# Linear attention and a feed-forward block in one planned program: loads, preparations and transposes get their own tokens in the order, and the order is rewritten

## The chip, the core and the metric

The kernel runs on one core of one Trainium2 chip. The metric is the device time of one execution in microseconds (us). The engines are named as the profile names them: PE is TensorE (its weight loads are PEld), DVE is VectorE, ACT is ScalarE, POOL is GpSimd, SP is SyncE, which here only issues DMAs.

## What is computed

Linear attention with a decay per head comes first, for 4 batches, 8 heads, 768 positions and 64 channels, in blocks of 64 positions; its output, laid out as 3072 tokens of 512 channels, goes through a feed-forward block of width 2048 with a "snake" activation. The reference, shortened:

```python
for b in range(nb):                       # 12 blocks of 64 positions
    intra = einsum(qb, kb) * Dmask        # decay lam ** (i - j), causal
    out[b] = intra @ vb + (qb * lam_pow) @ kv_state
    kv_state = lam_block * kv_state + (kb * rev_pow).T @ vb
x = out.transpose(0, 2, 1, 3).reshape(3072, 512)
h = x @ w_in                              # 512 -> 2048
g = h + sin(alpha * h) ** 2 / (alpha + 1e-9)
y = g @ w_out                             # 2048 -> 512
```

## The kernel before

**Units and chunks.** A unit is 256 positions of one batch with all 8 heads; there are 12 units, 0 to 11, and two units make a chunk of 512 tokens, of which there are 6. For each unit three loads bring q, k and v as float32 (`load_unit`, issued on SP in halves for units 0 and 1 and whole, 512 KB each, after that). Each of the three has two halves by head group, and `uscale` prepares each half: k is cast to bfloat16 (line 509), q and v are multiplied by a table of powers of lam (line 523). Units 0 to 3 are then transposed by PE into a PSUM bank and copied out (`upiece_T`, lines 539 and 548); units 4 to 11 are transposed by a DMA that SP issues (`upiece_D`, line 555).

**Attention pieces.** Line 578 issues the small matmuls of the attention: scores S, sums Z for the state, and outputs O. DVE masks the scores into `Smu` (lines 658 and 767) and adds the state `Zs` (671 and 778); the state is cast into `Zu` (674 and 781); O is cast into `xT`, the feed-forward input (688 and 788). For units 4 on, `upair` joins the S and Z of one unit with the O of the unit before; it uses seven of the eight PSUM banks.

**Feed-forward.** An A piece makes 512 columns of PSUM with four matmuls of 128x512 (`unit_A`, line 811) or with eight of 128x256 (`unit_A2`, line 845, written h in the order). ACT takes the sine (821 and 855), POOL or ACT the square (826 and 860, or 825 and 859), and DVE multiplies and adds into `gT` (828, and 863 twice for an h), which also frees the bank. A B piece is four matmuls of 128x512 (`unit_B`, line 876); four of them, written b chunk.tile.quarter, make 128 tokens of output, which ACT copies (890) and stores. There are 96 A pieces and 96 B pieces. The weights arrive by DMAs on POOL's queue, the first 512 columns of w_in by SP as float32 (`ws`) with a cast (line 424).

**What sets the order.** `_Plan` records every operation with a guessed length, its reads and its writes, and then picks operations one by one: the one that can start first, and among those the one recorded first. `HEAD` is the list for units 0 and 1. `ORDER` is a list of tokens for the rest: a and h make an A piece, b a B piece, s passes over a free bank, g makes the next attention piece. Loads, preparations (`uprep`, all six halves of a unit) and DMA transposes of units 4 on are recorded by the list `ahead`, in a fixed sequence, as soon as enough attention pieces have been made. An operation with several possible engines goes to the one that the plan sees finished first, after an addition per engine. Until 26 us of the plan, PE's waits are filled with idle matmuls (line 950).

## Time and profile before

| what | value |
|---|---|
| median of 3 runs | 216.12 us (216.10 to 216.44) |
| profiled execution | 216.58 us |
| its span in the profile | 214.8 us |
| time outside the span | 1.78 us |
| PE, DVE, ACT, POOL busy | 205.0, 136.6, 143.5, 93.9 us |
| DMA read and written | 27.28 MB, 6.29 MB |

The page has the busy time of each engine, then the span in 40 slices, the chain that ended last, and groups of instructions by line. An "idle before" with an arrow names what released the engine. A busy PE row ends where its pipelined last matmul is modelled to end, so rows of PE that follow each other overlap by some 0.17 us.

### The profile page before, as it was taken

How to read it: one execution, taken by the hardware profiler on the slowest of the kernel's cores; microseconds unless marked ns; L12 is line 12 of the kernel's file. 1: busy time of each engine (PE TensorE's matmuls, PEld its weight loads, DVE VectorE, ACT ScalarE, POOL GpSimd, SP SyncE). 2: the span in 40 equal slices, each digit the busy share in tenths (PEclk: the TensorE clock that was granted, in tenths of full speed). 3: DMA queues.
4: the chain of work that ended last, by engine and by line, in shares of the span. 5: the costliest groups of instructions: out<-in, count | busy, mean ns of one | idle time of the engine just before them, and what ended most of it. 6: DMA issues, size and time to landing. Idle time of an engine off the chain costs nothing.

```text
span 214.8 us, 5435 instructions
## 1 busy us (share of the span) xinstructions
PE 205.0 (95%) x2290; PEld 114.9 (53%) x2290; DVE 136.6 (64%) x225; ACT 143.5 (67%) x264; POOL 93.9 (44%) x106
## 2 busy tenths in 40 slices
PE   4999998999997998999999999999999999999995
PEld 1355756455644755547655558855454444444454
DVE  2697677796779964969985557846656556543000
ACT  2466887655788835777955867937758699686141
POOL 2555573752759656447985405912300530110000
PEclk9999999999999999999999999999999999999999
DMA  4999999999999999999999815011011000001134
GB/s 108 298 309 234 206 255 258 252 265 344 297 202 289 271 179 318 178 283 218 277 251 268 99 49 101 2 42 62 0 52 49 0 0 3 0 2 49 52 146 148
DMA packets 62986, 34.45 MB, mean 160 GB/s; under 512 B 18273, under 2 KB 60017, under 8 KB 62961
## 3 DMA queue, kind: packets, MB, share of 16 engines
q1 hardware_dynamic: 55632, 24.25, 50.3%
q0 software_dynamic: 3696, 3.67, 10.3%
q10 hardware_dynamic: 3632, 6.17, 8.6%
q8 instruction: 18, 0.29, 0.6%
q14 instruction: 8, 0.06, 0.1%
HBM read 27.28 MB, written 6.29 MB: 156 GB/s over the span
## 4 chain that ended last, share of the span: by engine, by line
PE 78%; DMA 11%; POOL 3%; SPq 3%; ACT 2%; issue 1%; DVE 0%; POOLq 0%
PE bank L876 38%; PE bank L811 18%; PE bank L845 13%; PE bank L578 7%; DMA w<-in_moe_w_in_dram 5%; DMA k<-in_k_dram 3%; SPq L385 3%; DMA q<-in_q_dram 3%; POOL u L826 2%; PE bank L539 1%; POOL w L385 1%; ACT t L821 1%; POOL qkv L523 1%; ACT osb L890 0%; DVE gT L828 0%
## 5 line engine op out<-in xcount | busy, mean ns | idle before, releaser
L876 PE MATMUL bank<-w,gT 128*128 128x512 bf16 (+1 forms) x400 | 89.6, 371 | 1.0 <-ACT osb L890 0.7
L876 PEld LDWEIGHTS bank<-w,gT 128*128 128x128 bf16 x400 | 38.0, 98 | 41.6 <-ACT osb L890 1.2
L828 DVE SCALAR_TENSOR_TENSOR gT<-u,rinv,bank 128x512 bf16<-128x512 bf16 x56 | 40.7, 744 | 22.0 <-ACT u L825 13.4
L811 PE MATMUL bank<-xT,w 128*128 128x512 bf16 x224 | 53.1, 379 | 0.8 <-DVE gT L828 0.5
L821 ACT ACTIVATE t<-bank,alpha 128x512 bf16<-128x512 f32 x56 | 37.4, 685 | 12.2 <-PE bank L811 11.4
L863 DVE SCALAR_TENSOR_TENSOR gT<-u,rinv,bank 128x256 bf16<-128x256 bf16 x80 | 34.3, 475 | 12.8 <-POOL u L860 7.3
L845 PE MATMUL bank<-xT,w 128*128 128x256 bf16 x320 | 38.7, 273 | 0.2 <-DVE gT L828 0.2
L855 ACT ACTIVATE t<-bank,alpha 128x256 bf16<-128x256 f32 x80 | 32.9, 474 | 6.6 <-PE bank L845 5.0
L811 PEld LDWEIGHTS bank<-xT,w 128*128 128x128 bf16 x224 | 21.5, 98 | 25.7 <-DVE gT L828 1.0
L845 PEld LDWEIGHTS bank<-xT,w 128*128 128x128 bf16 x320 | 30.5, 98 | 8.2 <-ACT xT L788 1.5
L860 POOL TENSOR_TENSOR u<-t 128x512 bf16<-128x512 bf16 x25 | 26.0, 1056 | 17.8 <-ACT t L855 17.7
L826 POOL TENSOR_TENSOR u<-t 128x512 bf16<-128x512 bf16 x19 | 20.2, 1069 | 29.9 <-ACT t L821 19.6
L890 ACT COPY osb<-bank 128x512 f32<-128x512 f32 (+1 forms) x25 | 14.2, 568 | 21.9 <-PE bank L876 21.9
L767 DVE TENSOR_TENSOR Smu<-bank,masku 128x1024 bf16<-128x1024 f32 x16 | 18.9, 1219 | 13.6 <-PE bank L578 13.6
L825 ACT ACTIVATE u<-t 128x512 bf16<-128x512 bf16 x37 | 23.3, 630 | 1.8 <-DVE gT L828 0.6
L523 POOL TENSOR_TENSOR qkv<-v,Lv 128x512 bf16<-128x512 f32 x15 | 17.4, 1167 | 12.8 <-PE bank L578 10.9
L523 POOL TENSOR_TENSOR qkv<-q,Lq 128x512 bf16<-128x512 f32 x13 | 15.0, 1159 | 11.5 <-DMA q<-in_q_dram 11.5
L788 ACT CAST xT<-bank 128x512 bf16<-128x512 f32 x14 | 9.8, 740 | 9.5 <-PE bank L578 9.5
L950 PE MATMUL bank<-masku,ident 128*128 128x512 bf16 x33 | 11.2, 452 | 2.7 <-DVE masku L461 2.7
L658 DVE TENSOR_TENSOR Smu<-bank,masku 128x1024 bf16<-128x1024 f32 x8 | 9.7, 1223 | 3.3 <-PE bank L578 3.2
L509 ACT CAST qkv<-k 128x512 bf16<-128x512 f32 x11 | 6.8, 617 | 6.0 <-DMA k<-in_k_dram 6.0
L578 PE MATMUL bank<-qkT,Zu 64*64 64x128 bf16 x160 | 10.3, 221 | 0.3
(55 smaller groups left out, 142.0 us busy)
## 6 DMA issues: line engine op xcount, KB each, us to landing
out_dram<-osb ACTq DMA_DIRECT2D x23, 256.0 KB, 2.1
k<-in_k_dram SPq DMA_DIRECT2D x10, 512.0 KB, 6.5
q<-in_q_dram SPq DMA_DIRECT2D x10, 512.0 KB, 7.2
v<-in_v_dram SPq DMA_DIRECT2D x10, 512.0 KB, 8.0
w<-in_moe_w_out_dram POOLq DMA_DIRECT2D x4, 512.0 KB, 9.4
w<-in_moe_w_in_dram POOLq DMA_DIRECT2D x3, 512.0 KB, 11.4
k<-in_k_dram SPq DMA_DIRECT2D x4, 256.0 KB, 5.4
v<-in_v_dram SPq DMA_DIRECT2D x4, 256.0 KB, 5.4
```

The lines of the kernel that those rows point to most:

```text
L523: emit = lambda e: e.tensor_tensor(dst, src, tab, ALU.mult)
L578: ins = e.matmul(to, w, x, start=(b, c) not in seen, stop=True, skip_group_check=True)
L811: ins = e.matmul(ps[hb][:, c0:c1], w1[:, kc, 128 * m:128 * (m + 1)], xT[x][:, kc, c0:c1], start=(kc == 0 and c0 == lo), stop=(kc == NKC - ...
L821: op("ACT", lambda e: e.activation(t16[ju][:, w], ps[hb][:, w], ACTF.Sin, scale=alpha[:, m:m + 1]), 0.69 * f, [bank(hb), "alpha"], [("t16" ...
L825: lambda e: (e.activation(u16[ju][:, w], t16[ju][:, w], ACTF.Square) if e is nc.scalar else e.tensor_tensor(u16[ju][:, w], t16[ju][:, w], ...
L826: e.tensor_tensor(u16[ju][:, w], t16[ju][:, w], t16[ju][:, w], ALU.mult)), 0,
L828: op("DVE", lambda e: e.scalar_tensor_tensor(out=gT[g][:, m, w], in0=u16[ju][:, w], scalar=rinv[:, m:m + 1], in1=ps[hb][:, w], op0=ALU.mul ...
L845: ins = e.matmul(ps[hb][:, 256 * i:256 * i + 256], w1[:, kc, 128 * (m + i):128 * (m + i + 1)], xT[x][:, kc, lo:lo + 256], start=(kc == 0 a ...
L855: op("ACT", lambda e, i=i: e.activation(t16[ju][:, 256 * i:256 * i + 256], ps[hb][:, 256 * i:256 * i + 256], ACTF.Sin, scale=alpha[:, m + ...
L860: e.tensor_tensor(u16[ju][:, :], t16[ju][:, :], t16[ju][:, :], ALU.mult)), 0,
L863: op("DVE", lambda e, i=i: e.scalar_tensor_tensor(out=gT[g][:, m + i, lo:lo + 256], in0=u16[ju][:, 256 * i:256 * i + 256], scalar=rinv[:, ...
L876: ins = e.matmul(ps[ob][:, w], gT[g][:, m, 128 * s4:128 * (s4 + 1)], w2[:, m, w], start=(m == 0), stop=(m == NM - 1),)
```

## The change

Numbers for the planner: later or shorter landings of unit loads, 0.9 us in place of 0.68 us for a q or v scale on DVE from unit 2 on, 1.1 us in place of 1.05 us on POOL, 1.8 us and 3.2 us in place of 1.45 us and 2.5 us for a DMA transpose. The additions that steer an operation away from an engine come from a list, `late_by`, set by a token G in `HEAD`. The list `ahead` goes; in its place the order has tokens l (next unit's loads), p (next unit's preparation) and d (next unit's two DMA transposes). `HEAD` and `ORDER` are new.

```diff
-                        lat=(2.7 if u < 4 else 5.0) if g is None else 2.9, ...
+                        lat=(2.7 if u < 2 else 3.7 if u < 4 else 3.9) if g is None else 2.9, ...
-            HEAD = """lk00 lv00 lq00 lk01 k01:POOL lv01 lq01 v01:POOL q00:POOL lk10 k00:DVE ...
+            HEAD = """lq01 lk00 lv00 lv10 v00:POOL k00:POOL lq00 lv01 Tk00:2ACT v01:POOL lk01 q01:DVE G:-1,7,8,2,6,6,12
-                    long = {"POOL": 1.05 if u > 1 else 1.1, "DVE": 0.68}
+                    long = {"POOL": 1.1, "DVE": 0.9 if u > 1 else 0.68}
-                op("SP", lambda e: e.dma_start_transpose(qkT[:, sl, :, :], flat), 1.45,
+                op("SP", lambda e: e.dma_start_transpose(qkT[:, sl, :, :], flat), 1.8,
...
-                   dma=f"qkT{sl}", runs=16, lat=2.5, issue=1.3)
+                   dma=f"qkT{sl}", runs=16, lat=3.2, issue=1.3)
-                        op((("ACT", 0.4, 0.0), ("POOL", 0.4, 0.0)),
+                        op((("ACT", 0.4, late_by[6]), ("POOL", 0.4, 0.0)),
-                        op((("ACT", 0.74, 0.4), ("DVE", 0.72, 0.0)),
+                        op((("ACT", 0.74, late_by[5]), ("DVE", 0.72, 0.0)),
-                op((("POOL", 1.05 * f, 0.0), ("ACT", 0.6 * f, 0.2)),
+                op((("POOL", 1.05 * f, 0.0), ("ACT", 0.62 * f, late_by[0])),
-                op((("POOL", 1.05, 0.0), ("ACT", 0.6, 0.3)),
+                op((("POOL", 1.05, 0.0), ("ACT", 0.62, late_by[1])),
-            ORDER = """h0.1.6 h0.1.0 b0.0.0 h0.1.2 h0.0.6 a0.4 b0.2.0 a0.5 h0.1.14 h0.1.8 s s s h0.0.14 s s g ...
+            ORDER = """p h0.1.0 a0.4 s s h0.1.2 a0.5 g a0.6 a0.7 b0.2.0 b0.0.0 s h0.1.8 s s h0.1.14 h0.0.8 s s ...
-                    uscale(u, which, g, (("ACT", 0.2), ("POOL", 0.0), ("DVE", 0.5)) if which == "k" else (("POOL", 0.0), ("DVE", 0.5)))
+                    uscale(u, which, g, (("ACT", late_by[2]), ("POOL", 0.0), ("DVE", late_by[3])) if which == "k" else (("POOL", 0.0), ("DVE", late_by[4])))
-                while ahead and ahead[0][0] <= done:
-                    ahead.pop(0)[1]()
+                elif kind == "l":
+                    load_unit(next(loads), "kqv")
+                elif kind == "p":
+                    uprep(next(preps))
+                elif kind == "d":
+                    u = next(turns)
+                    upiece_D(u, "k")
+                    upiece_D(u, "q")
```

Three places show what this does to the engines. The first is PE at the end of the head, where the feed-forward begins. L578 is the attention of unit 1, L950 (L961 after) an idle matmul, L845 and L811 are A pieces, L876 a B piece. Before:

```order
L578 MATMUL bank<-qkT 64x128 x16
L950 MATMUL bank<-masku,ident 128x512
L845 MATMUL bank<-xT,w 128x256 x8
L578 MATMUL bank<-Smu,qkv 64x128 x16
L578 MATMUL bank<-qkT,Zu 64x128 x4
L578 MATMUL bank<-Smu,qkv 64x128 x16
L578 MATMUL bank<-qkT,Zu 64x128 x4
L845 MATMUL bank<-xT,w 128x256 x32
L811 MATMUL bank<-xT,w 128x512 x4
L876 MATMUL bank<-w,gT 128x512 x4
```

And now:

```order
L578 MATMUL bank<-qkT 64x128 x16
L961 MATMUL bank<-masku,ident 128x512 x7
L578 MATMUL bank<-Smu,qkv 64x128 x16
L578 MATMUL bank<-qkT,Zu 64x128 x4
L961 MATMUL bank<-masku,ident 128x512
L578 MATMUL bank<-Smu,qkv 64x128 x16
L578 MATMUL bank<-qkT,Zu 64x128 x4
L845 MATMUL bank<-xT,w 128x256 x24
L811 MATMUL bank<-xT,w 128x512 x8
L845 MATMUL bank<-xT,w 128x256 x8
```

The A piece that stood ahead of unit 1's last two attention outputs has moved behind them, and eight idle matmuls stand there instead of one.

The second place is POOL's queue in the head, with the semaphores that each row waits for; dma_uq11 is the landing of q, unit 1, second half, and ws0 and ws256 are the two parts of the first w_in columns. Before:

```order
L385 DMA w1<-in_moe_w_in_dram 128x4x512 [waits dma_uq11]
L385 DMA w2<-in_moe_w_out_dram 128x4x512
L385 DMA w1<-in_moe_w_in_dram 128x4x512 [waits dma_uv11]
L523 TENSOR_TENSOR qkv<-v32_1,Lv 128x512 [waits dma_uv10]
L385 DMA w1<-in_moe_w_in_dram 128x4x512 [waits dma_ws256]
L385 DMA w2<-in_moe_w_out_dram 128x4x512
```

And now:

```order
L523 TENSOR_TENSOR qkv<-q32_1,Lq 128x2x4x64 [waits dma_uq10]
L385 DMA w1<-in_moe_w_in_dram 128x4x512
L523 TENSOR_TENSOR qkv<-q32_1,Lq 128x2x4x64 [waits dma_uq11]
L385 DMA w1<-in_moe_w_in_dram 128x4x512
L385 DMA w1<-in_moe_w_in_dram 128x4x512 [waits dma_ws0]
L385 DMA w2<-in_moe_w_out_dram 128x4x512
L523 TENSOR_TENSOR qkv<-v32_1,Lv 128x512 [waits dma_uv11]
L385 DMA w2<-in_moe_w_out_dram 128x4x512
```

The first weight load has moved ahead; it is now the last quarter of w_in, `w1[3]`, for whose landing SP's load of unit 2 waits. The last v half of unit 1 is prepared behind four weight loads.

The third place is POOL around unit 4's scores, where units 5 and 6 are prepared. The digit of k32, q32 and v32 is the load buffer: 2 is unit 5 and 0 unit 6. Before:

```order
L860 TENSOR_TENSOR u16_0<-t16_0 128x512 [waits done_ACT]
L509 CAST qkv<-k32_2 128x2x4x64 [waits dma_uk2]
L523 TENSOR_TENSOR qkv<-q32_2,Lq 128x2x4x64 [waits dma_uq2]
L826 TENSOR_TENSOR u16_2<-t16_2 128x512 [waits done_ACT]
L826 TENSOR_TENSOR u16_1<-t16_1 128x512 [waits done_ACT]
L523 TENSOR_TENSOR qkv<-v32_2,Lv 128x512 [waits dma_uv2]
L826 TENSOR_TENSOR u16_3<-t16_3 128x512 [waits done_DVE,done_ACT]
L826 TENSOR_TENSOR u16_0<-t16_0 128x512 [waits done_DVE,done_ACT]
L826 TENSOR_TENSOR u16_2<-t16_2 128x512 [waits done_DVE,done_ACT]
L509 CAST qkv<-k32_0 128x2x4x64 [waits dma_uk0]
L523 TENSOR_TENSOR qkv<-q32_0,Lq 128x2x4x64 [waits dma_uq0]
```

And now:

```order
L860 TENSOR_TENSOR u16_1<-t16_1 128x512 [waits done_ACT]
L523 TENSOR_TENSOR qkv<-q32_2,Lq 128x2x4x64 [waits dma_uq2]
L860 TENSOR_TENSOR u16_0<-t16_0 128x512 [waits done_ACT]
L523 TENSOR_TENSOR qkv<-v32_2,Lv 128x512 [waits dma_uv2]
L860 TENSOR_TENSOR u16_2<-t16_2 128x512 [waits done_ACT]
L826 TENSOR_TENSOR u16_1<-t16_1 128x512 [waits done_ACT]
L826 TENSOR_TENSOR u16_3<-t16_3 128x512 [waits done_DVE,done_ACT]
L860 TENSOR_TENSOR u16_1<-t16_1 128x512 [waits done_ACT]
L781 CAST Zu_0<-Zs 128x256 [waits done_DVE]
L860 TENSOR_TENSOR u16_3<-t16_3 128x512 [waits done_ACT]
L860 TENSOR_TENSOR u16_1<-t16_1 128x512 [waits done_DVE,done_ACT]
L509 CAST qkv<-k32_0 128x2x4x64 [waits dma_uk0]
```

Unit 5's k is now prepared ahead of this stretch, its v ahead of most squares, and unit 6's k behind five more squares.

Over the whole program, counted in the order, POOL has 15 casts of k (10 before), 32 scales of q and v (28), 47 squares (44) and 14 casts of the state (9); ACT has 3 casts of k (11), 6 casts of the state (11) and 49 squares (52); DVE has 6 casts of k (3), 16 scales (20), and both casts of `ws`, which ACT had. A pieces of the h kind are 42 (40), of the a kind 54 (56). PE's matmuls are the same in number otherwise, but for 38 idle ones (33).

More of the change, by code (lines that the diff above doesn't have):

```diff
@@ L918, in _ @@
+            late, late_by = {}, [0.0] * 7
             for item in HEAD:
@@ L944, in _ @@
                     free = [int(x) for x in what]
+                elif kind == "G":
+                    late_by[:] = [int(x) / 10 for x in what.split(",")]
             load_w2(2, [last["w1", 2]])
@@ L979, in _ @@
                 outs_at[u - 1] = len(pieces) if u > U0 else outs_at[u - 1]
[L980 to L987 removed]
+            load_unit(2, "kqv", None, [last["w1", 3]])
+            load_w2(3, [last["k", 2]])
+            load_unit(3, "kqv")
+            loads, preps, turns = (iter(range(x, NU)) for x in (4, 2, UD))
             done, todo = 0, ORDER.split()
             for i, token in enumerate(todo):
[L990 to L991 removed]
                 kind, arg = token[0], [int(x) for x in token[1:].split(".") if x]
@@ L1023, in _ @@
                         free.append(held.pop((c, t)))
-            assert done == len(pieces) and not ahead
+            assert done == len(pieces)
             P.filler = (spin, ("masku", "ident"), 26.0)
```

63 lines of the change are left out of this document (31 added, 32 removed).

## The prediction

> **What bounds it now.** First the page: which engine is full, and what the last chain is made of.
>
> ```profile
> PE 205.0 (95%) x2290; PEld 114.9 (53%) x2290; DVE 136.6 (64%) x225; ACT 143.5 (67%) x264; POOL 93.9 (44%) x106
> PE 78%; DMA 11%; POOL 3%; SPq 3%; ACT 2%; issue 1%; DVE 0%; POOLq 0%
> ```
>
> PE is busy for 95% of the span and makes 78% of the chain; the DMA share is the head, before the feed-forward can begin. So the time is a start, then PE's fixed work, then PE's stalls, then the tail. The timeline of PE dates the start and the first wait for unit 2, the chain the end:
>
> ```profile
> 19.84 1.04 PE L845 MATMUL bank<-xT,w 128*128 128x256 bf16 x8
> 22.08 3.73 PE L845 MATMUL bank<-xT,w 128*128 128x256 bf16 x32
> ...
> 34.69 0.61 PE L539 MATMUL bank<-ident,qkv 128*128 128x128 bf16 x8 [0.55 <-ACT qkv L509]
> ...
> 124.66 3.45 PE bank L876 x16
> ...
> 195.75 16.46 PE bank L876 x92
> ```
>
> One A piece runs at 19.84; from 22.08 to 195.75 + 16.46 = 212.21 (190.1 us) PE runs the other 191 pieces and the attention of units 2 to 11. Four pieces take 3.45 us, so one takes 0.863. The stretches and PE's own waits behind 35 us show where it stalls:
>
> ```profile
> 22.00:35.14 13.14, 12.23 (x91) 8.06 (x92) 9.35 (x20) 10.41 (x22) 7.66 (x8) 1.00 1.20 244
> ...
> 55.73:75.00 19.27, 17.86 (x178) 11.10 (x177) 16.91 (x27) 16.88 (x34) 13.88 (x15) 1.00 1.19 260
> 75.00:95.00 20.00, 19.06 (x288) 10.31 (x287) 13.94 (x24) 12.45 (x24) 11.30 (x13) 1.00 1.15 238
> ...
> PE bank L876 <- ACT osb L890: 0.7, 1, 0.7
> PE bank L811 <- DVE gT L828: 0.5, 1, 0.5
> PE bank L578 <- DVE gT L863: 0.4, 1, 0.4
> PE bank L811 <- issue: 0.3, 1, 0.3
> PE bank L578 <- DVE gT L828: 0.2, 1, 0.2
> PE bank L845 <- DVE gT L828: 0.2, 1, 0.2
> ```
>
> The columns are the stretch's length, then the busy time of PE, PEld, DVE, ACT and POOL. PE is short by 1.41 us in 55.73:75 and by 0.94 us in 75:95, with six waits (2.3 us). A wait really costs some 0.17 us more than its idle time, since the row ahead of it ends late by that (19.84 + 1.04 reaches past the 0.865 us of its eight matmuls): 2.35 + 6 x 0.17 = **3.4 us behind 35 us**. From 22.08 to 35.14 PE does 13 pieces and one transpose (0.45): 11.7 us in 13.06, so **1.3 us of stalls** there. In all 4.7 us can be won; the fixed work is 190.1 - 4.7 + 0.9 (the piece at 19.84) + 0.1 (its change of kind) = 186.4 us, and the tail is 214.8 - 212.2 = 2.6 us. If X is the start of the unbroken feed-forward with all 192 pieces ahead, **span = X + 189.0 + stalls**.
>
> **The head: where X comes to lie.** SP's first loads land one after the other:
>
> ```profile
> 0.81 0.45 SPq L385 DMA_DIRECT2D k<-in_k_dram  x1
> 10.84 1.71 SPq L385 DMA_DIRECT2D ws<-in_moe_w_in_dram  x2
> ...
> k<-in_k_dram SPq DMA_DIRECT2D x1, 256.0 KB, 4.7
> ws<-in_moe_w_in_dram SPq DMA_DIRECT2D x1, 512.0 KB, 6.0
> ...
> 10.81 0.42 DVE L669 COPY Zs<-bank 128x256 f32<-128x256 f32 x1 [0.88 <-PE bank L578]
> 11.15 1.22 DVE L658 TENSOR_TENSOR Smu<-bank,masku 128x1024 bf16<-128x1024 f32 x1
> 11.30 0.40 POOL L674 CAST Zu<-Zs 128x256 bf16<-128x256 f32 x1
> ...
> 14.21 0.69 DVE L548 COPY qkT<-bank 128x1024 bf16<-128x1024 bf16 x1
> ...
> 21.35 0.46 PE L578 MATMUL bank<-Smu,qkv 64*64 64x128 bf16 x16
> ```
>
> The first lands at 0.81 + 4.7 = 5.5, the first `ws` at 10.84 + 6.0 = 16.84, 13 places of 256 KB later: 0.87 us a place. In the new list k of unit 1, second half, is in place 13 (15.9 us), v in place 14 (16.8, or 17.4 because the weight loads, begun earlier, now share the wire), and `ws0` in places 11 and 12 (15.1). DVE casts `ws0` and then k (16.4; 0.45 a cast, below); PE's transpose (0.61, the row at 34.69) and the copy (0.69) reach 17.8, with the hand-overs. The first scores end at 18.3. The v half is scaled on POOL at 17.4 + 1.04 = 18.5, so Z (some 0.45, as the output rows) runs to 19.0 and the second scores to 19.5. On DVE follow `Smu` (1.22) from 18.4, `Zs` (0.42) and `Smu` (1.22) to 21.3. An output takes 0.73, from 21.35 to the A pieces at 22.08 in before: the second starts at 22.0 and **X = 22.8** (22.1 to 23.6: v at its place, or delayed by a whole one). Against before this is 0.7 us later and without the early piece: 1.6 us lost.
>
> What may win it back is that the weights begin earlier:
>
> ```profile
> 13.89 0.94 POOL L385 DMA_DIRECT2D w<-in_moe_w_in_dram  x1 [2.19 <-DMA q<-in_q_dram]
> ...
> w<-in_moe_w_in_dram POOLq DMA_DIRECT2D x1, 512.0 KB, 7.9
> ...
> w<-in_moe_w_out_dram POOLq DMA_DIRECT2D x1, 512.0 KB, 9.5
> ...
> 26.97 0.37 SPq L385 DMA_DIRECT2D k<-in_k_dram  x1
> ...
> k<-in_k_dram SPq DMA_DIRECT2D x1, 512.0 KB, 6.9
> ...
> k<-in_k_dram SPq DMA_DIRECT2D x1, 512.0 KB, 13.1
> ```
>
> The load at 13.89 needs 7.9 us; the new first one goes out at 12.7 (q of place 8 at 11.6, plus its scale) and lands at 20.6. The second, issued behind it at 14.8, took 9.5 us to 24.3, 2.5 behind the first, so the new second, `w1[1]`, is due at some 23.1 to 23.7; it is needed at 22.8 + 3 x 0.865 = 25.4. SP's k of unit 2 then goes out 6.4 us earlier than at 26.97. It took 6.9 us with few weight loads beside it and 13.1 us (unit 3's) with more: it lands at 27.5 to 33.7, and I take 31.5, between them, since four weight loads are still due. The A pieces need it transposed at 22.8 + 13 x 0.865 = 34.1, so the wait at 34.69 goes. Unit 2's q and v come later behind it and both halves are scaled on two engines at once, which costs 0.5 us (below): I charge 0.6 us for the two, 0 to 1.5. With 0.1 for the first B piece this makes **0.7 us of stalls up to unit 2's Z**, where before had 1.3. The head as a whole loses 1.6 - 0.6 = 1.0 us.
>
> **Collisions of DVE and POOL.** Two pairs of rows, and the prices by kind:
>
> ```profile
> 45.81 0.69 DVE L523 TENSOR_TENSOR qkv<-q,Lq 128x512 bf16<-128x512 f32 x1
> 45.85 1.55 POOL L523 TENSOR_TENSOR qkv<-q,Lq 128x512 bf16<-128x512 f32 x1 [1.06 <-DMA q<-in_q_dram]
> ...
> 53.84 1.04 POOL L523 TENSOR_TENSOR qkv<-q,Lq 128x512 bf16<-128x512 f32 x1
> 53.95 1.48 DVE L523 TENSOR_TENSOR qkv<-q,Lq 128x512 bf16<-128x512 f32 x1
> ...
> L509 ACT CAST qkv<-k 128x512 bf16<-128x512 f32 x11 | 6.8, 617 | 6.0 <-DMA k<-in_k_dram 6.0
> L860 POOL TENSOR_TENSOR u<-t 128x512 bf16<-128x512 bf16 x25 | 26.0, 1056 | 17.8 <-ACT t L855 17.7
> ```
>
> Whichever starts second is held: 1.55 in place of 1.04 on POOL, 1.48 in place of 0.69 on DVE. The old plan knew neither.
>
> **The middle.** In 55.73:75 before makes eleven A pieces around unit 4's scores while POOL also prepares units 5 and 6, and `gT` waits for squares. In the new order a B piece stands behind the first three, eight A pieces follow, and POOL has unit 6's k behind five more squares. Followed with the rows' lengths, the last `gT` before the scores frees its bank 0.6 us too late; I count **0.6 us** where 1.41 + 4 x 0.17 = 2.1 stood (0 to 2.1).
>
> In 75:95 the largest wait is for ACT's copy of an output (0.7). The new order has a wait there too, but ACT loses eight casts of k (0.617 each) and five of the state (0.40, as on POOL): 6.9 us over the program. Half of 0.94 + 2 x 0.17 = 1.3 stays, **0.6 us** (0 to 1.3). Behind 95 us before has almost no stall to give.
>
> POOL takes on 5 casts of k (0.61, nearest ACT's 0.617), 4 scales (1.04 to 1.55), 5 casts (0.40) and 3 squares (1.056): 3.1 + 4.2 to 6.2 + 2.0 + 3.2, some 13 us on 93.9. In 55.73:75 it is busy for 13.88 of 19.27 us; the work spread over 55 to 125 us costs nothing while squares come in time. Not in the trace: `ws` cast on DVE. ACT's took 1.05 us; I take 0.7, in proportion to DVE's k cast (at most 0.45 for half the size, so up to 0.9); either way it ends before `Smu`, and costs nothing. The idle matmuls lie in waits.
>
> **The sum.** 22.8 + 189.0 + 0.7 + 0.6 + 0.6 = **213.7 us** of span, 1.1 less than 214.8. The profiled execution took 216.58, 1.78 outside the span, which the change doesn't touch; against the median of 216.12 the same step gives **215.0 us**.
>
> **The rivals.**
>
> *The stalls stay and the head is lost.* The plan's lengths were made finer but the engines still drift from it: with X as above and 4.7 us of stalls, 22.8 + 189.0 + 4.7 = 216.5, median 217.8. For it speaks that the start moves behind two more attention outputs, against it that the largest stall was at a known collision. It decides against the change from 3.0 us of stalls on, where the span is 214.8.
>
> *POOL becomes the bound.* Squares go late, banks stay taken, PE waits. If a fifth of POOL's added 13 us comes to lie on PE's path beside the forecast's stalls, that is 2.6 us: 217.6. POOL's idle time ahead of squares (17.8 us for the h kind) speaks against it.
>
> *Gains and losses cancel.* Some 1.1 us of the new waits for unit 2 and its like come on top: 216.1, no change.
>
> *All stalls behind X go:* 22.8 + 189.0 = 211.8, median 213.1.
>
> *The casts on DVE hold up the weights.* Three squares of POOL at 66.05 take 3.03 us, so two take 2.02; the two at 104.57 take 2.22, while DVE casts k at 105.44:
>
> ```profile
> 66.05 3.03 POOL L826 TENSOR_TENSOR u<-t 128x512 bf16<-128x512 bf16 x3
> ...
> 104.57 2.22 POOL L826 TENSOR_TENSOR u<-t 128x512 bf16<-128x512 bf16 x2
> 105.44 0.45 DVE L509 CAST qkv<-k 128x512 bf16<-128x512 f32 x1
> ```
>
> So a cast holds POOL for about 0.2 us, up to its whole length. Two `ws` casts beside the five weight loads could set those back by 0.2 to 0.9 each; `w1[1]` has 1.7 us or more to spare, so only if both losses fall on it (1.8) and its own landing is at the late end does PE wait, and then for the next weights as well: up to 0.9 us, 215.9. [...]
>
> **Chances.** Forecast 0.40, all stalls gone 0.10, cancelled 0.13, the casts 0.05 (also no change), stalls stay 0.22, POOL 0.10. A measurement of this kernel can tell about 0.2%, 0.43 us, from no change. Faster 0.50, same 0.18, slower 0.32. The forecast's own range is 214.2 to 215.7. The range for 8 in 10 reaches from 213.1, with all stalls gone, to 217.8, with all kept; X's bounds move the forecast to 214.3 and 215.8, inside it.
>
> **What would show it.** The first dense A pieces at 22.8; SP's load of unit 2 at 20.6; no wait of PE for unit 2's k, and short ones for its q and v; PE idle in the twenty us around unit 4's scores under 1 us; POOL near 107 us busy, ACT near 137. It is wrong if X is beyond 23.6, if PE's waits behind 35 us still sum to over 2.3 us, or if PE waits for squares of POOL in the last chunks.

## The result, and the profile after

The changed kernel is slower: median **218.28 us** of nine runs (216.78 to 218.65) against 216.12 us of nine runs of the kernel before (215.96 to 216.99), a ratio of 1.0079 with a 95% interval of 1.0053 to 1.0105. Forecast was 215.0 us, with 213.1 to 217.8 for 8 in 10. Two of the nine runs lie at 216.8, the other seven at 217.8 to 218.7. The execution profiled first took 218.65 us with a span of 216.7 us, 3.0 us more than the 213.7 us of the forecast. A second and a third profile of the same kernel, r1 and r3 below, took 217.11 us (span 215.2) and 218.49 us (216.6). The mean granted clock is 0.999 or 1.0 in all runs told of here but r2, a single run whose time is therefore not compared, three of e5's four (the fourth took 223.01 us), and two of e10's seven, which its times below leave out.

The page, with the busy times and the chain that ended last:

```profile
PE 207.1 (96%) x2303; PEld 117.2 (54%) x2303; DVE 135.9 (63%) x224; ACT 136.8 (63%) x253; POOL 105.6 (49%) x123
PE 87%; DVE 4%; POOL 3%; DMA 2%; ACT 2%; issue 1%
```

ACT fell from 143.5 to 136.8 us and POOL rose from 93.9 to 105.6, as forecast (137 and 107); PE is still the full engine, and the DMA share of the chain, 11% in before, is 2%. The work went where the order sent it, and the time has to lie in PE's start and stalls. PE's timeline in the head, in the first profile and then in that of 217.11 us:

```profile
8.26 2.77 PE L961 MATMUL bank<-masku,ident 128*128 128x512 bf16 x6
10.82 0.63 PE L539 MATMUL bank<-ident,qkv 128*128 128x128 bf16 x4
...
18.94 0.62 PE L539 MATMUL bank<-ident,qkv 128*128 128x128 bf16 x8 [0.98 <-DVE qkv L509]
...
24.61 2.82 PE L845 MATMUL bank<-xT,w 128*128 128x256 bf16 x24
```

```profile
7.61 1.46 PE L961 MATMUL bank<-masku,ident 128*128 128x512 bf16 x6
10.05 0.40 PE L539 MATMUL bank<-ident,qkv 128*128 128x128 bf16 x4 [0.99 <-DVE qkv L523]
...
23.29 2.82 PE L845 MATMUL bank<-xT,w 128*128 128x256 bf16 x24
```

The unbroken feed-forward begins at 24.61 us in the one and at 23.29 us in the other, where X = 22.8 was forecast. The same six idle matmuls take 2.77 us in the first and 1.46 us in the second (0.43 and 0.22 us each, leaving out the overlap): PE still ran at half its rate at 10 us in the first, though the granted clock of the rows is 1.00 in both. There the transpose of unit 0's second q half, whose operand DVE had written at 10.03, stood behind them until 10.82. What a late transpose does next, DVE beside POOL in the first profile:

```profile
13.80 1.06 POOL L523 TENSOR_TENSOR qkv<-q,Lq 128x512 bf16<-128x512 f32 x1
...
13.93 1.22 DVE L509 CAST qkv<-k 128x512 bf16<-128x512 f32 x1
...
16.33 1.19 POOL L385 DMA_DIRECT2D w<-in_moe_w_out_dram  x1
...
17.14 1.75 DVE L509 CAST qkv<-k 128x512 bf16<-128x512 f32 x1
...
17.54 1.06 POOL L523 TENSOR_TENSOR qkv<-v,Lv 128x512 bf16<-128x512 f32 x1
```

And DVE's same two casts in the second:

```profile
12.92 0.42 DVE L509 CAST qkv<-k 128x512 bf16<-128x512 f32 x1
...
15.93 0.43 DVE L509 CAST qkv<-k 128x512 bf16<-128x512 f32 x1 [0.20 <-DMA k<-in_k_dram]
```

A cast of 0.42 us takes 1.22 and 1.75 us here. The first starts 0.13 us behind a scale on POOL, the second during POOL's issue of a weight load and 0.40 us ahead of the next scale, and both end 0.29 us behind the end of that scale (14.86 and 18.60 us). The casts that r3 and e8 below have beside such a scale end 0.29 us behind it too, while in the second profile both casts run wholly beside issues of weight loads on POOL (from 12.84 and from 14.79 us) and are not held: it is the scale that holds them. They are the casts of unit 1's k, and PE waits 0.98 us for the second of them at 18.94.

The views behind the start, as in the prediction: PE's own waits, and the stretches around unit 4's scores and behind them, of the first profile:

```profile
PE bank L578 <- issue: 1.0, 1, 1.0
PE bank L876 <- ACT osb L890: 0.7, 1, 0.7
PE bank L876 <- ACT qkT L548: 0.2, 1, 0.2
PE bank L811 <- DVE gT L863: 0.2, 1, 0.2
```

```profile
57.70:77.00 19.30, 19.00 (x195) 12.52 (x193) 16.44 (x30) 16.49 (x34) 14.30 (x17) 1.00 1.20 250
77.00:97.00 20.00, 18.34 (x293) 10.89 (x292) 13.92 (x23) 10.22 (x20) 13.88 (x17) 1.00 1.06 236
97.00:167.00 70.00, 70.00 (x899) 40.73 (x896) 44.62 (x73) 48.26 (x92) 33.81 (x40) 1.00 0.53 117
```

Around unit 4's scores PE is short by 0.30 us where it was 1.41: the second term of the forecast came true. In the next twenty us it is short by 1.66 us where it was 0.94. ACT's output copy is there as before (0.7), and a new gap of 1.0 us "issue", in which PE waits for no semaphore. From 97 to 167 us nothing is lost. At the first A pieces of chunk 1, before was at 55.67 us with 32 pieces done, and the changed kernel is at 57.64 with 31: 1.97 + 0.86 = 2.8 us behind, of which it wins back 0.9 to be 1.9 behind at the end (216.7 against 214.8).

### The profile page after: what moved, and what is told of

It is laid out like the page before. It is cut to its first block, busy times and chain, and to the rows that moved or that the text cites. A ratio compares the mean times of both kernels' runs of the same rounds, so it can differ in the third digit from the quotient of the medians.

```text
span 216.7 us, 5443 instructions
## 1 busy us (share of the span) xinstructions
PE 207.1 (96%) x2303; PEld 117.2 (54%) x2303; DVE 135.9 (63%) x224; ACT 136.8 (63%) x253; POOL 105.6 (49%) x123
## 3 DMA queue, kind: packets, MB, share of 16 engines
q0 software_dynamic: 3696, 3.67, 10.1%
## 4 chain that ended last, share of the span: by engine, by line
PE 87%; DVE 4%; POOL 3%; DMA 2%; ACT 2%; issue 1%
PE bank L876 38%; PE bank L811 20%; PE bank L845 15%; PE bank L578 9%; PE bank L961 3%; POOL u L860 2%; DMA lam_bc<-in_lam_dram 2%; PE bank L539 2%; DVE qkv L509 1%; POOL qkv L523 1%; DVE Smu L658 1%; ACT t L855 1%; ACT qkT L548 0%; ACT osb L890 0%; DVE gT L863 0%
## 5 line engine op out<-in xcount | busy, mean ns | idle before, releaser
L876 PE MATMUL bank<-w,gT 128*128 128x512 bf16 (+1 forms) x400 | 89.7, 371 | 0.9 <-ACT osb L890 0.7
L876 PEld LDWEIGHTS bank<-w,gT 128*128 128x128 bf16 x400 | 38.2, 98 | 42.2 <-issue 1.2
L828 DVE SCALAR_TENSOR_TENSOR gT<-u,rinv,bank 128x512 bf16<-128x512 bf16 x54 | 38.8, 744 | 26.5 <-ACT u L825 20.6
L811 PE MATMUL bank<-xT,w 128*128 128x512 bf16 x216 | 50.9, 379 | 0.2 <-DVE gT L863 0.2
L863 DVE SCALAR_TENSOR_TENSOR gT<-u,rinv,bank 128x256 bf16<-128x256 bf16 x84 | 35.8, 475 | 15.5 <-POOL u L860 13.4
L860 POOL TENSOR_TENSOR u<-t 128x512 bf16<-128x512 bf16 x31 | 32.3, 1054 | 22.0 <-ACT t L855 22.0
L855 ACT ACTIVATE t<-bank,alpha 128x256 bf16<-128x256 f32 x84 | 35.0, 476 | 10.0 <-PE bank L845 9.5
L845 PE MATMUL bank<-xT,w 128*128 128x256 bf16 x336 | 40.5, 273 | 0.0
L845 PEld LDWEIGHTS bank<-xT,w 128*128 128x128 bf16 x336 | 32.0, 98 | 7.9 <-ACT xT L788 0.9
L811 PEld LDWEIGHTS bank<-xT,w 128*128 128x128 bf16 x216 | 20.7, 98 | 24.7 <-DVE gT L863 0.9
L826 POOL TENSOR_TENSOR u<-t 128x512 bf16<-128x512 bf16 x16 | 16.7, 1041 | 26.0 <-ACT t L821 25.5
L767 DVE TENSOR_TENSOR Smu<-bank,masku 128x1024 bf16<-128x1024 f32 x16 | 18.9, 1219 | 11.9 <-PE bank L578 11.9
L523 POOL TENSOR_TENSOR qkv<-v,Lv 128x512 bf16<-128x512 f32 x18 | 19.5, 1096 | 8.7 <-PE bank L578 7.7
L961 PE MATMUL bank<-masku,ident 128*128 128x512 bf16 x38 | 13.3, 478 | 2.7 <-DVE masku L461 2.7
L781 POOL CAST Zu<-Zs 128x256 bf16<-128x256 f32 x12 | 5.1, 433 | 18.5 <-DVE Zs L778 12.7
L509 POOL CAST qkv<-k 128x512 bf16<-128x512 f32 x15 | 9.9, 676 | 5.2 <-DMA k<-in_k_dram 5.2
```

What stands on the lines that cost most here:

```text
L523: emit = lambda e: e.tensor_tensor(dst, src, tab, ALU.mult)
L811: ins = e.matmul(ps[hb][:, c0:c1], w1[:, kc, 128 * m:128 * (m + 1)], xT[x][:, kc, c0:c1], start=(kc == 0 and c0 == lo), stop=(kc == NKC - ...
L828: op("DVE", lambda e: e.scalar_tensor_tensor(out=gT[g][:, m, w], in0=u16[ju][:, w], scalar=rinv[:, m:m + 1], in1=ps[hb][:, w], op0=ALU.mul ...
L845: ins = e.matmul(ps[hb][:, 256 * i:256 * i + 256], w1[:, kc, 128 * (m + i):128 * (m + i + 1)], xT[x][:, kc, lo:lo + 256], start=(kc == 0 a ...
L855: op("ACT", lambda e, i=i: e.activation(t16[ju][:, 256 * i:256 * i + 256], ps[hb][:, 256 * i:256 * i + 256], ACTF.Sin, scale=alpha[:, m + ...
L860: e.tensor_tensor(u16[ju][:, :], t16[ju][:, :], t16[ju][:, :], ALU.mult)), 0,
```

## The experiments

### Which half of the change loses: e4, e5, e13

The new body behind the old head, and the other way round:

```diff
-            HEAD = (the new list)                     # e4
+            HEAD = (the list of before) + G:-1,7,8,2,6,6,12
-            HEAD = (the list of before)               # e5, in the kernel before
+            HEAD = (the new list, without G)
```

> The old list for units 0 and 1 (HEAD) with the new order of the rest, its tokens and planner numbers. Theory 1 (the loss lies in the head): start as in the kernel before, the body's smaller stalls stay, 214.6 to 215.6 us. Theory 2 (the body loses): 217 us or more.

> The new list for units 0 and 1 with the old order of the rest, its fixed sequence of loads and preparations and its planner numbers. Theory 1: dense A pieces start at some 24.6, and the time is 218.5 to 219.5 us, since the old body's stalls come on top of the late start. Theory 2: 216.0 to 216.8 us, as before.

e4 took 216.49 us (216.37 to 217.49, ten runs), 1.0022 of before (1.0011 to 1.0034), with a span of 214.7. e5 took 224.96 us, 1.0378 of before (1.0328 to 1.0429); its PE waits 2.9 us at one transpose for a `gT`. Both missed the ranges of both theories: e4 lies between them, and e5 is beyond the slower one by 3.5 us or more in every run, so the new head costs more with the old body than with the new one. Taking back HEAD alone brings 1.8 of the 2.2 us back: **behind the new body, the loss comes with the new head**. But the new body behind the old head wins nothing either; it loses 0.4 us. In e4 PE waits for a quarter of w_in and three more things:

```profile
PE bank L845 <- DMA w<-in_moe_w_in_dram: 1.1, 1, 1.1
PE bank L811 <- ACT xT L788: 0.8, 1, 0.8
PE bank L876 <- DVE qkT L548: 0.8, 1, 0.8
PE bank L876 <- ACT osb L890: 0.7, 1, 0.7
```

e13 exchanges two tokens so that the quarter which is there first is asked for first:

```diff
-  ... b0.2.0 b0.0.0 s h0.1.8 s s h0.1.14 h0.0.8 ...
+  ... b0.2.0 b0.0.0 s h0.1.14 s s h0.1.8 h0.0.8 ...
```

> The new body behind the old head, as in e4, with two A pieces of the order exchanged (columns 1792 on before columns 1024 on), since the old head brings the last quarter of w_in first. On each engine the sequence of instructions is the same as in e4. If the wait of 1.1 us for w_in was a real loss: no such wait, span 213.3 to 214.0, time 215.0 to 215.8, so 0.2 to 0.5% faster than before. Rival (the time is taken up by the next wait, for qkT and osb): span 214.3 or more, time 216.0 to 216.5, as e4.

It missed: 216.57 us, and PE still waits 1.0 us for w_in at 29.5 us (e4: 29.4), and 1.1 us for `xT` at 129 us (e4: 0.8). What the new body would be worth behind a head that suits it stays open.

### What makes the start late: e1, e3, e7, r1, r3, e9, e10, e11

e1 gives unit 1's k to ACT, e3 plans idle matmuls with the length they have while PE is slow, e7 does both:

```diff
-  ... k10:DVE ... k11:DVE ...                  # e1, e7
+  ... k10:ACT ... k11:ACT ...
-        each = 0.4 if at < 8.0 else 0.24       # e3, e7
+        each = 0.43 if at < 12.0 else 0.24
```

> The changed kernel, with unit 1's two casts of k on ACT in place of DVE. Theory 1 (the head lost its time because DVE's casts of k were held by POOL, 1.22 and 1.75 us in place of 0.43): the dense A pieces start at 23.0 to 23.6 in place of 24.6, and the time falls by 1.0 to 1.6 us, to some 216.7 to 217.3. Theory 2 (the new order of the body loses the time, the head's start is made up for later): within 0.4 us of the changed kernel's 218.3.

> The changed kernel, with the idle matmuls before 12 us counted at 0.43 us each, as the trace shows them, so that one fewer stands ahead of the transpose of q. Theory 1 with its side cause (idle matmuls overrun and push the whole chain of the head by 0.8 us): the start of the dense A pieces comes 0.3 to 0.9 us earlier, the time falls as much. Against it: the casts that POOL holds end when POOL lets go, so an earlier chain waits longer there and the start moves by less than 0.2 us.

> The changed kernel with both mends of its head: unit 1's k cast by ACT, and idle matmuls planned with 0.43 us up to 12 us. Theory 1 (DVE's casts held by POOL and idle matmuls too long each cost part of the 1.8 us by which the start was late): dense A pieces at 22.3 to 22.8, span 214.5 to 215.5 without a gap of the instruction stream, time 216.3 to 217.4; with gaps up to 2.5 us more. Rival (the start is set by the landings of k and v, and each mend alone has already reached them): A pieces at 22.8 to 23.0, as with either alone.

e1 starts its dense A pieces at 23.01 us, e3 at 22.79 (22.8 was the forecast for the change), e7 at 23.50 (22.3 to 22.8 was expected). No cast of k is held in any of them. In e3 and e7 PE kept its low rate until about 9.9 and 11.7 us, and the start is still earlier than in the first profile, as theory 1 says; e1's PE was at its full rate by 7.6 us, where the changed kernel itself can start at 23.29, so e1's start shows little. The times don't follow: e1 218.14 us (ratio 1.0110, 1.0059 to 1.0160), e3 218.76 (1.0107, 1.0069 to 1.0145), e7 217.22 (1.0056, 1.0039 to 1.0073). **A start that is 1.1 to 1.8 us earlier bought between nothing and 1.1 us.**

r1 and r3 are the changed kernel again:

> The changed kernel once more, unchanged, for a second profile. Its nine times lie at 216.8 (two) and 217.8 to 218.7 (seven). Theory F (part of the spread is the late block of PE's instructions, 0.98 us in the first profile): the start of the dense A pieces is again at 24.5 to 24.7, and the time follows the gaps of PE that wait for nothing but their instructions: a run near 216.8 has none or only a short one near 88 us, a run near 218.5 has about 1 us. Rival: the gap has the same length in a run that is over 1 us faster or slower.

> The changed kernel unchanged, a third profile. Start at 23.1 to 23.5 if PE leaves its slow clock before 10 us, 24.4 to 24.7 if behind 11 us; a packet of PE's instructions that starts by 84 us leaves no gap, one that starts at 85.5 us or later leaves a gap of 1 us or more. Rival: start or gap do not follow these two marks.

r1 (217.11 us) started at 23.29, not at the 24.5 to 24.7 expected, and had no gap near 88 us; r3 (218.49 us) started at 24.65 with a gap of 0.81 (1 or more expected). Start and gap went together, as in the first profile. PE had left its low rate by 6.6 us in r1, and only behind 11 us in the other two. Before the first transpose PE has a pause of 0.8 us in all three. e9 fills it with two more idle matmuls and moves nothing else; e11 makes such a pause in the kernel before:

```diff
-        n = int((t - best[0]) / each)
+        n = int((t - best[0]) / each) + (2 if at < 3.5 else 0)    # e9; - in place of + in e11
```

> The changed kernel with nine idle matmuls in place of seven at the very start, so that PE has no pause before its first transpose (0.8 us in the two profiles of the changed kernel); nothing else differs on any engine. Theory C (the start moves with the time at which PE leaves its slow clock: in the profile with the start at 24.6 the idle matmuls took 0.43 us each until 11.2 us, in the one with the start at 23.3 they took 0.22 us from 6.6 us on; the pause decides which): the transpose of unit 0's second q half runs at 10.0 to 10.3, the A pieces start at 23.2 to 23.5, and all times lie at 216.8 to 217.3, none at 218 or above unless a block of instructions is late. Rival (the two groups of times have another cause, as the order in which DVE and POOL start): times still spread over 216.8 to 218.6.

> The kernel before with five idle matmuls in place of seven at the start, so that it has a pause of some 0.9 us there as the changed kernel has; nothing else differs. Theory C: PE leaves its slow clock later in some runs (behind 9 us in place of 7), and some of the times are 0.3 to 1.5 us longer than 216.1, in a second group; the A pieces of those start later than 22.1. Rival (the head of before waits for its landings and hides a slow PE): times stay at 215.9 to 216.4.

e9's A pieces start at 23.07 us, and its five times spread over 0.3 us only, 218.08 to 218.41. e16 below, with the same head, starts at 23.26. With the pause the changed order started at 24.61 and 24.65, but also at 23.29 (r1) and 23.19 (e12): so the late start comes with the pause, though not always, and two profiles can't show that it never comes without. Theory C's 216.8 to 217.3 us failed, but for the exception that it made, a late block of instructions: the start is 1.5 us earlier than in the first profile and the time is the same. Its waits show the block (1.0, with 0.17 us more); without it some 217.1 us would be left, by estimate:

```profile
PE bank L578 <- issue: 1.0, 1, 1.0
PE bank L539 <- POOL qkv L523: 0.7, 1, 0.7
PE bank L876 <- ACT osb L890: 0.7, 1, 0.7
PE bank L578 <- DVE gT L863: 0.4, 1, 0.4
PE bank L876 <- ACT qkT L548: 0.2, 1, 0.2
PE bank L811 <- DVE gT L863: 0.2, 1, 0.2
```

e11 says the same of the kernel before: its profile starts the dense pieces at 22.73 in place of 22.08 us, the span is 214.4 (before 214.8), and the median is 216.12 us against 216.11, ratio 1.0001 (0.9987 to 1.0016). A start 0.65 us later cost it nothing. Four of its twelve times lie at 216.8 to 216.9; three of the 21 of before lie at 216.7 to 217.0, so the second group that theory C foresaw isn't clear of what before does itself. e10 mends the head further (no pause, real lengths, fewer idle matmuls behind 17 us, k on ACT):

> The changed kernel with its head mended in four ways: no pause before the first transpose, idle matmuls planned with 0.43 us up to 12 us and with 0.40 us behind 17 us (so that four and not seven stand ahead of unit 1's first output), and unit 1's k cast by ACT. Theory (the head's loss is made of these): A pieces at 22.0 to 22.6, span 213.9 to 214.8, time 215.6 to 216.6. Rival (the landings of k and v and DVE's chain of masks set the start): A pieces at 22.8 or later, time 216.8 or more.

It reached X = 22.37 us, the earliest of all, in a run of 218.50 us that has a gap of 1.25 us at 54 us; its five times are 217.06 to 219.72 us, median 217.13 (ratio 1.0072, 1.0036 to 1.0109). The theory was right on the start and wrong on the time (215.6 to 216.6), and e10's three fastest, 217.06 to 217.13, are no faster than r1 with its start at 23.29. A start that is not what the later pieces wait for buys nothing. The first output of unit 2 (the next matmuls of line 578 on `Smu`) shows it, from PE's timeline in the twelve profiles that have the changed kernel's order behind the head:

| start X, us | kernels | unit 2's first output, us |
|---|---|---|
| 24.61, 24.65, 24.73 | changed (twice), e15 | 49.82, 49.86, 49.83 |
| 23.50, 23.29, 23.26, 23.19 | e7, r1, e16, e12 | 49.20, 49.41, 49.48, 49.27 |
| 23.07, 23.01, 23.01 | e9, e1, e3 again | 49.38, 49.58, 49.48 |
| 22.79, 22.37 | e3, e10 | 49.58, 49.51 |

From 24.7 to 22.4 us the start moves by 2.3 us and this output by 0.7 at most, and below 23.5 not at all. In the first profile PE waits only 0.2 us between the two, so there the start still dates the output; below 23.5 something else does. With the old head, in e4, it runs at 47.55, with the same 25 pieces ahead of it.

### What holds unit 2: e15, e16

In r1 PE waits 0.27 us for unit 2's q and 0.65 us for its v. DVE's rows there, and the rows of before:

```profile
33.62 0.76 DVE L509 CAST qkv<-k 128x512 bf16<-128x512 f32 x2 [0.25 <-DMA k<-in_k_dram]
...
39.26 0.69 DVE L523 TENSOR_TENSOR qkv<-q,Lq 128x512 bf16<-128x512 f32 x1 [0.55 <-DMA q<-in_q_dram]
...
43.45 0.69 DVE L523 TENSOR_TENSOR qkv<-v,Lv 128x512 bf16<-128x512 f32 x1 [0.30 <-DMA v<-in_v_dram]
```

```profile
33.93 0.43 DVE L509 CAST qkv<-k 128x512 bf16<-128x512 f32 x1 [0.51 <-DMA k<-in_k_dram]
36.77 0.69 DVE L523 TENSOR_TENSOR qkv<-q,Lq 128x512 bf16<-128x512 f32 x1
...
41.90 1.04 POOL L523 TENSOR_TENSOR qkv<-v,Lv 128x512 bf16<-128x512 f32 x1 [1.54 <-DMA v<-in_v_dram]
```

SP issues unit 2's k at 21.92 us in r1 and at 26.97 in before. Issued 5.05 us earlier, k lands 0.3 us earlier (33.6 against 33.9), q at least 2.5 us later (39.3 against 36.8 or less) and v 1.6 us later (43.5 against 41.9). The DMA engines, the wire of these texts, were busy throughout in both: DMA share and GB/s are the last two columns, of before and of r1,

```profile
18.00:24.00 6.00, 5.66 (x96) 3.68 (x87) 4.10 (x7) 4.32 (x8) 1.26 (x3) 1.00 1.23 206
24.00:30.00 6.00, 6.00 (x46) 4.21 (x45) 4.15 (x9) 5.37 (x12) 4.66 (x5) 1.00 1.24 210
30.00:36.00 6.00, 5.09 (x38) 2.92 (x35) 4.15 (x9) 4.58 (x11) 3.00 (x4) 1.00 1.16 287
```

```profile
18.00:24.00 6.00, 5.32 (x120) 3.02 (x120) 4.27 (x7) 1.40 (x3) 1.32 (x2) 1.00 1.23 206
24.00:30.00 6.00, 5.95 (x42) 3.89 (x41) 3.40 (x8) 5.33 (x12) 4.68 (x5) 1.00 1.21 212
30.00:36.00 6.00, 5.95 (x50) 4.29 (x48) 5.11 (x11) 4.51 (x10) 5.05 (x6) 1.00 1.19 235
```

so loads issued earlier only stand longer beside the weights, and from 30 to 36 us less comes in (235 against 287 GB/s). In that stretch the weights' queue moved 0.73 MB in r1 and 0.30 in before. Two runs took one neighbour each off the wire, with all engines' orders as in e9 but for e15's setting of zeros on POOL:

```diff
-                    w2[:, ...], moe_w_out[...].rearrange(...)                 # e15: third and fourth quarter
+                    w2[:1, ...], moe_w_out[...].rearrange(...)[:1]
-                        dst, src[...].rearrange(...)                          # e16: unit 3
+                        dst[:1], src[...].rearrange(...)[:1]
```

> The kernel without the pause at the start (e9), but the third and fourth quarter of w_out bring one partition in place of 128, the rest of them is zero, set on POOL before its first cast; this leaves most of half of w_out out of the computation. Theory L (these loads hold back unit 2's q and v): q lands before 38 us in place of 39.5, v before 42 in place of 43.4, PE's wait of 0.74 us for unit 2's q is gone, the first output of unit 2 runs at 48.7 or earlier in place of 49.4, and the time is 0.6 to 1.0 us below e9's 218.2 if the late block of instructions stays. Rival (SP's own queue is slow): q at 39 or later and the same wait.

> The kernel without the pause at the start (e9), but the loads of unit 3 bring one partition in place of 128; the rest of unit 3 is computed from unit 0's values, which is left out of the computation so. They are issued behind unit 2's on the same queue. If that queue serves its loads in turn, unit 2's q and v land as before, at 39.5 and 43.4, and the waits and the time (218.2, or 217.0 if the late block of instructions disappears) stay; if it serves them together, q and v land 1 us or more earlier and the wait of 0.74 us for q is gone.

e16 took 218.32 us. Its q is prepared at 39.02 us (r1 39.26, e9 39.51) and its v at 43.51, as in r1 and e9; PE's wait for q is gone and that for v grew to 0.9 us. So unit 3's loads are not what makes v late, as if the queue served its loads in turn. e15 took 219.18 us: setting the zeros on POOL moved the start to 24.73, so PE waited for neither q nor v, and what their landing is worth isn't seen in the time. But the DMA view dates the landings. Unit 2's load of v, issued at 22.95 us in r1 and at 22.56 in e15, with its time to landing at the end:

```profile
v<-in_v_dram SPq DMA_DIRECT2D x1, 512.0 KB, 20.5
```

```profile
v<-in_v_dram SPq DMA_DIRECT2D x1, 512.0 KB, 15.0
```

It lands at 43.5 us in r1 and at 37.6 in e15; q, issued at 21.93 and 14.0 us under way, lands at 35.9 in e15, where r1's is waited for until 39.3. The two late loads of w_out thus cost q some 3 us and v nearly 6: on the landings theory L holds. And in all nine profiles with X up to 23.5 POOL stands idle for 1.3 to 1.9 us until v has landed, in the three with X above 24.6 not at all; where PE's own wait there names a `gT` (e3, e7, e9), that `gT` stands on DVE behind the scale of v. So below 23.5 it is the landing, and not the start, that dates unit 2. An earlier start feeds this: r1's POOL issues the two w_out loads at 28.28 and 33.89 us, that of the first profile at 29.61 and 34.78, and there v lands at 41.1. What an early start and an early landing together are worth, no run shows.

### The gap in which PE waits for nothing: r2, e8, e12

PE's timeline at the gap in the first profile, and the packet of the instruction queue that the DMA view has from 85.8 to 86.0 us:

```profile
87.22 0.29 PE L578 MATMUL bank<-qkv 64*64 64x64 bf16 x7
88.50 0.19 PE L578 MATMUL bank<-qkv 64*64 64x64 bf16 x1 [0.98 <-issue]
```

```profile
q8 instruction: 1, 0.02, 37.9%
```

The whole execution has 18 such packets (0.29 MB, so 16 KB each) for 2303 matmuls and as many weight loads, so one per 128 matmuls, or 256 instructions. The trace's rows say the same: counted in matmuls, weight loads and PE's few semaphore rows, this gap stands behind the 2241st, the gaps of e1 and e10 near 54 us behind the 1217th, and one in the head of r1 and e9 (0.45 and 0.73 us, behind 19 us) behind the 449th, so 4 x 256 and 3 x 256 apart. That such a packet brings a block of 256 of PE's instructions is worked out from these counts. Two attention pairs, of 96 and 112 small matmuls and 5 us apart, stand here, so PE runs through a block in about 5 us and not in the 28 us (128 x 0.216, a quarter of a piece's 0.863) of dense work. When this packet comes decides:

| kernel | packet starts, us | gap of PE behind it, us |
|---|---|---|
| e12, e7, r1 | 82.4, 82.5, 83.5 | none |
| e3 | 85.6 | none |
| e9, r3, e16, changed, e15 | 85.6, 85.8, 85.8, 85.9, 85.9 | 1.0, 0.8, 1.2, 1.0, 1.1 |
| e10 | 87.1 | none |
| e1 | 87.5 | 1.0 |
| r2 | 88.4 | 2.65 |

The packets with a gap behind them take 1.0 to 1.2 us, and in every such gap PE goes on 1.3 to 1.6 us behind the packet's end: in the first profile at 88.50, where the packet ended at 87.17. So there is a gap when PE reaches the place sooner than that. In e3 and e10 it gets there about in time, at 88.1 and 89.5 us, 1.2 us behind the packet's end: both have fewer idle matmuls, so that the block's border lies further on in their order. The fourth packet before it does the same: it starts at 47 to 50 us in the other profiles of this order, and at 51.9 in e1 and 51.3 in e10, which alone have gaps of 1.6 and 1.25 us at 52 to 54 us. Before has 0.27 us at the same place of PE's program (packet at 86.7, and dense pieces behind it). r2 is e3 again:

> The kernel that plans idle matmuls with their real length, unchanged, for a second profile. Its profiled run took 217.3 and had no gap of PE's instruction stream; its other three took 218.5 to 219.1. Theory F: in a run near 218.8 PE has 1 to 2 us of gaps that wait for nothing the profile shows, and the A pieces start at 22.8 again; in a run near 217.3 it has none. Rival: the start or the waits for other engines differ by the 1.2 to 1.8 us.

It started at 23.01 us (e3: 22.79) and had the gap that e3 lacked, so theory F's mark holds; and, in this one run, it shows a second price:

```profile
90.81 5.32 PE L845 MATMUL bank<-xT,w 128*128 128x256 bf16 x32 [2.65 <-issue]
```

The 32 matmuls behind the gap take 5.32 us, where they take 3.67 us in r1; the granted clock from 90.8 to 96.2 us is 0.68, and 1.00 before the gap. PE ran slower for a while after it had stood still. e8 and e12 ask whether full DMA engines make the packet late:

```diff
-                    load_unit(next(loads), "kqv")                        # e8
+                    u = next(loads); load_unit(u, "kqv") if u < 7 else None
-                        dst, src[...].rearrange(...)                     # e12
+                        dst[:1 if u > 6 else 128], src[...].rearrange(...)[:1 if u > 6 else 128]
```

> Left out: the loads of q, k and v of units 7 to 11; these units are computed from what the buffers held before. All else is the changed kernel's. Theory F (the 0.98 us gap of PE at 88 us is a block of its instructions that comes late because the DMA engines are full of loads): the DMA share falls from 9 tenths to under 5 behind some 70 us, the gap near 88 us is under 0.2 us, the start stays at 24.5 to 24.7, the span is 215.4 to 216.0 and the spread of the times shrinks to under 1 us. Rival (the gap comes from PE itself or from the profile): the gap of 1.0 us stays and the span is 216.5 or more.

> The changed kernel's order on every engine, but the loads of q, k and v of units 7 to 11 bring one partition in place of 128; the rest of these units is computed from what the buffers held before, which is left out of the computation so. Theory F (late blocks of PE's instructions, up to 2.65 us in one gap, come from DMA engines full of loads): no gap of PE without a cause behind 70 us over 0.3 us, DMA share under 6 tenths there. The start is as in the changed kernel, 23.3 or 24.6, so the times lie at 216.0 to 217.6. Rival (the gap has nothing to do with the loads): gaps of 1 us or more near 88 us in the profile, and times up to 218.6 as before.

e8 is no clean test: with the loads gone from the plan, the plan placed other work, and the kernel got waits of 1.1 and 0.9 us for `xT` (219.66 us); of the gap nothing was left. e12 keeps the order on every engine. Its waits, and its stretch 72:100:

```profile
PE bank L876 <- ACT osb L890: 0.7, 1, 0.7
PE bank L578 <- POOL qkv L523: 0.7, 1, 0.7
PE bank L876 <- ACT qkT L548: 0.2, 1, 0.2
PE bank L811 <- DVE gT L863: 0.2, 1, 0.2
PE bank L539 <- POOL qkv L523: 0.2, 1, 0.2
```

```profile
72.00:100.00 28.00, 27.32 (x454) 17.60 (x452) 21.61 (x35) 16.42 (x33) 21.33 (x25) 1.00 0.55 103
```

At half the DMA share (0.55, the first profile has 1.10 there) the gap is gone, and the five times are 216.84 to 217.56 us, 217.23 in the median. Against e9, which starts at the same time (23.07; e12 23.19) and has the gap, that is 1.0 us. So the late block costs about 1 us, and in e8 and e12, on a light wire, there is none. That a full wire alone makes it isn't shown, since r1 and e7 escape it at a share of 1.18; what makes the packet late in one execution and not in another stays open.

## Why the prediction was wrong, point by point

**The sum held, its terms did not.** Span = X + 189.0 + stalls, each wait at its idle time + 0.17 us. First profile: 24.6 + 189.0 + 0.4 (`qkT`) + 0.4 (`gT`) + 2.0 (the gap and `osb`) = 216.4, measured 216.7. r1: 23.3 + 189.0 + 1.7 (q, `qkT`, v) + 0.4 + 0.9 = 215.3, measured 215.2.

**The step that failed first is "the head: where X comes to lie", and with it "unit 2's q and v come later behind it ... I charge 0.6 us".** X came at 23.3 to 24.65 us for 22.8. The working had DVE cast k in 0.45 us at 16.4, and "the idle matmuls lie in waits". In the first profile the casts took 1.22 and 1.75 us behind POOL's work, and idle matmuls stood ahead of a transpose whose operand was there. The hold of DVE by POOL was priced in the prediction by rows of the trace, but only for places of the body, and the head's were not followed on both engines at once. The idle matmuls were put at nothing, though PE's low rate at the start is in before too (seven of them in 3.17 us, from 2.74). In r1, where no cast was held, X is 0.5 us beyond the forecast, about as much as the gap of 0.45 us in its head. X alone is 1.8 of the 3.0 us in the first profile, but less than that was lost by it. Where X came as forecast (e3, 22.79) the span was 215.5 and not 213.7, since unit 2's q and v held PE for 2.0 us with `qkT` (0.80, 0.23, 0.48 and 3 x 0.17) where 0.7 stood: the term for q and v was the mis-sized one. The prediction read SP's earlier issue as an earlier landing: k at 31.5 was forecast, 33.5 (21.58 + 11.9 us) came, so 6.4 us at the issue (5.4 in the profile) were worth 0.4 us. Of the bounds 27.5 to 33.7 the late one was true.

**The middle.** Around unit 4's scores 0.6 us was forecast and 0.4 came (0.22 + 0.17), where before had 2.1: the new lengths for DVE beside POOL do what they were read to do. In the following twenty us 0.6 was forecast and 2.0 came: the `osb` wait stayed whole (0.68 us, not half), although ACT was 6.7 us less busy, and the late block came on top. No step of the prediction looked at PE's instruction stream; the row of 0.3 us "issue" that it quoted was the sign.

**The rivals.** "The stalls stay and the head is lost" (217.8) was the nearest in time, and its point (3.0 us of stalls) about met: 2.9 to 3.1 in the three profiles. Its mechanism was not it: the stalls of before went, as forecast, and others came. POOL did not become the bound, and PE waits for no square of POOL in the last chunks. "The casts on DVE hold up the weights" had the right pair and the wrong victim: POOL's issue of a load took 1.19 us where 0.75 to 0.94 is usual, but DVE's cast, held by the scale behind that issue, took 1.3 us more. That a cast sets a weight load back by its whole length, the 0.9 us in this rival's 215.9, no run shows: the issue of 1.19 us, which had the `ws` cast of 0.68 us and the start of the cast of k beside it, was 0.25 to 0.44 us longer than usual. Nor does "whichever starts second is held", read in the prediction from two pairs of rows, give both casts: the first started 0.13 us behind the scale and waited, the second 0.40 us ahead of the scale and waited too.

**The signs.** POOL near 107 (105.6), ACT near 137 (136.8), PE idle under 1 us around unit 4's scores (0.30), and no wait for unit 2's k: right. SP's load of unit 2 at 20.6 (21.58 and 21.92) and X at 22.8: wrong. Of the signs of being wrong, X beyond 23.6 came in two of three profiles; PE's waits behind 35 us sum to 2.1 us in the first, just under the 2.3 set for them.

## What to carry to other kernels

Before an earlier start is counted as a gain or a late one as a loss, look for what dates the next stage: here loads on a full wire did, and 2.3 us at the start were worth 0.7 us or less there, and 0.65 us nothing in the kernel before. A load that is issued earlier on a full wire need not land earlier (issued 5.05 us earlier, at a DMA share of 1.16 to 1.24, k landed 0.3 us earlier here); take its landing from bytes and shares, not from the issue plus the shortest row. Where many small matmuls stand close together, see in the DMA view when the packets of PE's instructions start: here seven of the nine that started at 85.6 us or later left a gap of 0.8 to 2.65 us.

## What the runs showed of the hardware that was not expected

PE's rate at the start differs between executions of one kernel: full by 6.6 us in r1, and from about 11.4 us in the first profile. The granted clock of the rows shows 1.00 in both. In the ten profiles of the new head with the pause the full rate came at 6.6 to 11.7 us, without the pause at about 5.8 (e16), 7.7 (e10) and 8.6 us (e9). What sets the time, no run shows.

A block of PE's instructions that comes late cost 0.8 to 2.65 us in one gap, at the same place of the program in seven profiles, and once (r2) 1.65 us more in the 32 matmuls behind it, at a granted clock of 0.68.

A DVE cast of 0.42 us took 1.75 us in the first profile, when it began during POOL's issue of a weight load and a scale on POOL followed; beside issues alone, in r1, it took 0.42 and 0.43.

Of two loads on SP's queue that r1 issued 5 us earlier than before, one landed only 0.3 us earlier (k) and one 1.6 us later (v); with two of POOL's weight loads cut to 4 KB (e15), v landed 5.9 us earlier than in r1.
